# A transformer block on one core: two more tiles for exponentials, the first block's second layer in two parts, gated products for 256 rows, and a later use of turned rows

## The chip, the cores and the metric

The kernel runs on one core of a Trainium2 chip. The time is that of the device in microseconds. Three executions of the kernel before took 905.71, 910.32 and 911.77 us; their median is 910.32. A core has TensorE (PE, matmuls), VectorE (DVE), ScalarE (ACT), GpSimd (POOL) and SyncE (SP, which issues the transfers here).

## The reference

The input x has 2048 rows of 640 numbers. Attention has 32 heads of 20 numbers, and the second layer is a product of two linear maps of width 1728.

```python
qkv = (x @ wqkv).reshape(B, S, 3, H, Dh).transpose(2, 0, 3, 1, 4)
q, k, v = qkv[0], qkv[1], qkv[2]
p = softmax(einsum("bhqd,bhkd->bhqk", q, k) * Dh ** -0.5)
A = einsum("bhqk,bhkd->bhqd", p, v).transpose(0, 2, 1, 3).reshape(B, S, D) @ wo   # A(x, wqkv, wo)
Bf = ((x @ w_gate) * (x @ w_up)) @ w_down                                         # B(x, ...)
h = x + A(layernorm(x), wqkv, wo)
out = h + B(layernorm(h), w_gate, w_up, w_down)
```

## The kernel before

The 2048 rows are four blocks of 512 (`QB`), and each block is four row tiles of 128. First every row tile is normalized and turned, so that the 640 columns lie on partitions (`lnT`); from that come the keys `kT`, the queries `qa` and `qb`, and the values `vx`. For a block other than the first the turning is a DMA transpose, issued by `turn` (L892) as soon as the tile is normalized; `T_of` (L897) is a job that holds back the jobs behind it until the planner's clock has passed the issue by `TURN_NS`.

The attention is a train of 683 score tiles. `emit_S` (L521) writes one score tile `sc` in PSUM, 128 keys by 1536 columns, of which there are two. Each column group belongs to one head, one tile of keys and a block (or half a block) of queries. ScalarE takes the exponential of the tile into a tile `E` in SBUF (L551), out of a pool of `E_BUFS` = 6. In some tiles the last 512 columns are computed by VectorE instead, in four instructions (L587 to L598, `xe`). `emit_AV` (L739) then multiplies E with the values and sums in the one PSUM bank `acc`; a tile of E is free again when its last such matmul is done.

Everything else is a job: a generator that yields after each matmul. The kernel is written by a planner that runs while the program is built. It keeps an estimated clock for TensorE, ScalarE and VectorE (`at`), and between two score tiles `run_job` (L503) issues as many steps of the first job as fit, in the order of a queue. A job can yield `WAIT`, and then stands in `waiting` while the next is tried (`step`, L404). Where nothing is to be done, `keep_warm` (L494) issues two matmuls of 512 columns without use, and L531 one. Every engine then runs its list in order; semaphores alone decide the real times.

When all heads of a block (or of half a block) are normalized (`due`, L1365), `add_tail` (L1215) queues the rest for these rows. `job_out` (L1045) multiplies by `wo` (L1012), adds x, normalizes, and turns the rows by DMA into `ln2T` (L1058). `job_glu` (L1149) computes, for seven groups of 256 columns, the up product u and the gate product, and their product `hh`; for 512 rows at once in `glu_sum` (L1109) and for 256 rows in `glu_two` (L1124). `job_y` (L1172) multiplies by `w_down` (L1179), adds, and stores. Block 0 goes through this with 512 rows in one part, blocks 1 to 3 with 256 rows in two. `open_late` (L976) opens the pools for these tiles in the space of the turned rows, when no query or key is left to be computed. The weights `wu` and `wg` have two tiles each, and are fetched anew for each part; for block 3 four of the seven groups are kept in the space of the old queries. The queries are spilled to HBM (L970) for a general path that this input doesn't take. The last 256 rows follow behind the last exponential (`last_tail`, L1269).

Of the kernel before, what the change touches and what calls it, by code (L numbers as in the profile page):

```python
# [64 lines left out]
LN_NS = 3300  # L65
TURN_NS = 2600
HOLD_AT, HOLD_NS = 5300, 450
# [5 lines left out]
PART_NS, TILE_NS, ROOM = 31500, 700, 2500  # L73
E_BUFS = 6
SHIFT = 544.0
# [13 lines left out]
def kernel(  # L89
# [250 lines left out]
    FINAL = len(segs) - 1  # L340
    TAILS = {0: [0], 1: [0, 2], 2: [0, 2]}
    FAST = {("E", NG - 1), ("F", NG - 1), ("C", NG - 1), ("D", NG - 1), ("A", NG - 1), ("B", NG - 2)}
# [61 lines left out]
    def step():  # L404
        if cur["fresh"] and (first() or waiting):
            if cur["gen"] is not None:
                jobs.appendleft((cur["key"], cur["gen"]))
            cur["key"], cur["gen"] = (urgent if first() else waiting).popleft()
        c = advance()
        if c == WAIT:  # L410
            waiting.append((cur["key"], cur["gen"]))
            cur["gen"] = None
            c = advance() if jobs and not any(w[0][1:] == jobs[0][0][1:] for w in waiting) else NEXT
        if c is None:
            return None
# [87 lines left out]
    def run_job(until):  # L503
# [15 lines left out]
        return at["pe"] > begun  # L519

    def emit_S(i):  # L521
        sc = scp.tile([P, EW], F32, name="sc")
# [24 lines left out]
        if start <= at["exp"] + X_LATE and x_takes(i):  # L547
            n_act = n - BANK
            took = emit_x(sc[:, n_act:n], [(s, kt, j, o - n_act) for s, kt, j, o in us if o >= n_act])
        e = ep.tile([P, EW], BF16, name="E")  # L550
        exps = nc.scalar.activation(e[:, 0:n_act], sc[:, 0:n_act], ACT.Exp, bias=EXP_BIAS, scale=SM_SCALE)  # L551
# [162 lines left out]
    def av_ns(upto):  # L714
        if not av_q or acc["seg"] not in (None, av_q[0][1]):
            return 0
        s = av_q[0][1]
        if acc["seg"] is None and at["pe"] < at["acc"] and now["i"] < acc["from"] and min(u[0] for u in av_q) > now["i"] - E_BUFS:
            return 0
# [6 lines left out]
        left = acc["left"] if acc["seg"] == s else END_OF_TIME  # L726
        if sum(rows) < min(most * HPG, left) and min(u[0] for u in av_q) > upto - E_BUFS + 3:
            return 0
# [10 lines left out]
    def emit_AV(upto):  # L739
# [9 lines left out]
        if acc["seg"] != s:  # L749
            if at["pe"] < at["acc"] and now["i"] < acc["from"] and min(u[0] for u in av_q) > now["i"] - E_BUFS:  # L750
                return
# [8 lines left out]
        ready = sum(len(r) for r in rows)  # L760
        if ready < min(most, acc["left"]) and min(u[0] for u in av_q) > upto - E_BUFS + 3:
            return
# [105 lines left out]
    def gen_ln(ch):  # L868
# [8 lines left out]
        for k, t in enumerate(ts):  # L877
            apply1(t, *made[0], k)
            done.add(("a", t))
            later(1, lambda t=t: turn(t))  # L880
            yield 780
# [10 lines left out]
    def turn(t):  # L892
        if t not in turned:
            nc.sync.dma_start(lnT[:, :, t * P:(t + 1) * P], lns[t], transpose=True)
# [13 lines left out]

    for ch in range(NB):
        def values(k=0, n=TPB):  # L910
            for t in range(ch * TPB + k, ch * TPB + n):
# [9 lines left out]
        else:  # L921
# [54 lines left out]
    def open_late():  # L976
# [132 lines left out]
    def glu_sum(st, fp, f2, k, c0, n, hold):  # L1109
        ps = bank()  # L1110
        for c in range(KT):
            nc.tensor.matmul(ps[:, 0:n], lhsT=st["w", fp][k][:, c, f_cols(fp, f2)],  # L1112
                             rhs=st["ln2T"][:, c, c0:c0 + n], start=(c == 0), stop=(c == KT - 1))
            if c == KT - 1:
# [3 lines left out]
                else:  # L1118
                    dve(605 if n == QB else 342, 216 * n // QB)
                    nc.vector.tensor_tensor(st["hh"][fp][:, f2, c0:c0 + n], ps[:, 0:n], hold["u"][:, 0:n], ALU.mult)  # L1120
            yield 216 * n // QB
        yield NEXT

    def glu_two(st, fp, c0, n, up_done):  # L1124
        u = late["s"].tile([P, QB], BF16, name="u")
        for k in range(2):
            ps = bank()
            for f2 in range(2):
                for c in range(KT):
                    nc.tensor.matmul(ps[:, f2 * n:(f2 + 1) * n], lhsT=st["w", fp][k][:, c, f_cols(fp, f2)],  # L1130
                                     rhs=st["ln2T"][:, c, c0:c0 + n], start=(c == 0), stop=(c == KT - 1))
                    if f2 and c == KT - 1:
# [3 lines left out]
                        else:  # L1136
                            two = lambda x: x.rearrange("p (f k) -> p f k", k=n)
                            nc.vector.tensor_tensor(st["hh"][fp][:, :, c0:c0 + n], two(ps[:, 0:2 * n]), two(u[:, 0:2 * n]), ALU.mult)  # L1138
                    yield 216 * n // QB
# [32 lines left out]
    def job_y(st, ts, store_halves=False):  # L1172
        for t in ts:
            o = st["xr"][t]
            for hf in range(2):
                ps = bank()
                cs = slice(hf * HALF, (hf + 1) * HALF)
                for f in range(2 * FP):
                    nc.tensor.matmul(ps[:, 0:HALF], lhsT=st["hh"][f // 2][:, f % 2, t * P:(t + 1) * P],  # L1179
                                     rhs=late["Wd"][f][:, cs], start=(f == 0), stop=(f == 2 * FP - 1))  # L1180
# [13 lines left out]
    IN_TURN = (0, 3, 1, 4, 2, 5, 6)  # L1194
    tail_st = {}
    held = []

# [17 lines left out]
    def add_tail(b, ts):  # L1215
        key = (b, ts[0])

        def ready():
            if key not in rows_in:
                rows(b, ts)  # L1220
            if b == 0:
                for fp in range(2):
                    later(4 * fp + 3, lambda fp=fp: load_w(fp, tail_st[b]))
# [24 lines left out]
        if b == 0:  # L1248
            for g in range(NG):
# [110 lines left out]
    def normed(p, gs):  # L1360
# [3 lines left out]
    first_last = next(k for k, (us, _) in enumerate(tiles) if PASS[segs[us[0][0]][0]][0] == LAST_B)  # L1364
    due = [("0", range(NG), 0, [0, 1, 2, 3]), ("E", range(SPLIT_G["1"], NG), 1, [0, 1]), ("F", range(SPLIT_G["1"], NG), 1, [2, 3]), ("C", range(SPLIT_G["2"], NG), 2, [0, 1]),  # L1365
           ("D", range(SPLIT_G["2"], NG), 2, [2, 3]), ("A", range(SPLIT_G["3"], NG), 3, [0, 1])]
    PARTS = [d[2:] for d in due]
    i = 0
    while i < n_tiles or av_q:
# [15 lines left out]
        for _ in range(2):  # L1385
            emit_AV(i if i >= n_tiles else i - 2 if i >= LAG else i - 3)
            if not av_q or min(u[0] for u in av_q) > i - E_BUFS + 1:
                break
# [116 lines left out]
```

## Time and profile before

| | |
|---|---|
| median of three executions | 910.32 us (905.71 to 911.77) |
| the profiled execution | 910.77 us, span 909.0 us |
| TensorE matmuls | 830.1 us busy, 91% of the span |
| ScalarE | 855.7 us busy, 94% |
| VectorE | 757.0 us busy, 83% |
| exponentials on ScalarE (L551) | 683, 838.2 us |
| moved by DMA | 57.50 MB, 63 GB/s in the mean |

Busy time counts overlapping instructions of one engine once. The page cuts the span into 40 slices of 22.7 us and gives the busy share of each engine and the granted clock of TensorE in tenths. A timeline row merges like instructions that follow each other without a gap; its name is that of the first, so a row of 93 exponentials holds both those of 1536 and those of 1024 columns.

### The profile page before, as it was taken

Reading aid. Unit: us, or ns where it says so; the run is one execution under the profiler, and the core shown is the slowest. Engines: PE = TensorE matmul, PEld = TensorE weight load, DVE = VectorE, ACT = ScalarE, POOL = GpSimd, SP = SyncE. Lnnn points to the kernel's source line nnn. Section 1 sums busy time; section 2 is a strip of 40 time slices with the busy share of each in tenths; the row PEclk is TensorE's granted clock in tenths of the full one; section 3 lists DMA queues with packets and bytes.
Section 4 is the critical chain, followed back from the end, with each engine's and each line's share of the span. In section 5 each row is a group of like instructions: output and inputs, shape, how many; then the busy total and the mean of one; then the engine's idle time right before and its main releaser. Section 6 shows DMA issues by size and latency. Waiting matters only on the chain.

```text
span 909.0 us, 21597 instructions
## 1 busy us (share of the span) xinstructions
PE 830.1 (91%) x8766; PEld 364.3 (40%) x8766; DVE 757.0 (83%) x1411; ACT 855.7 (94%) x719; POOL 35.1 (4%) x126
## 2 busy tenths in 40 slices
PE   8889999989998899999999998998999999989997
PEld 5233233222233223344444454433434544435565
DVE  7668899999999798889888899899888898875543
ACT  6999999999999899999999999999989999999951
POOL 4100000000002000001001000000000000010000
PEclk9999999999999899999999999999989999999999
DMA  6230010011034235411415134111453202011310
GB/s 196 58 59 1 1 31 21 14 37 27 14 103 101 54 116 162 113 44 37 108 31 122 36 102 99 45 30 43 113 136 92 64 13 74 16 28 40 85 44 18
DMA packets 107578, 57.50 MB, mean 63 GB/s; under 512 B 41833, under 2 KB 104469, under 8 KB 107473
## 3 DMA queue, kind: packets, MB, share of 16 engines
q1 hardware_dynamic: 107472, 56.06, 23.9%
q8 instruction: 70, 1.15, 0.5%
q14 instruction: 36, 0.29, 0.1%
HBM read 44.49 MB, written 7.28 MB: 57 GB/s over the span
## 4 chain that ended last, share of the span: by engine, by line
ACT 49%; PE 27%; issue 13%; DVE 9%; DMA 1%; SPq 0%; ACTq 0%; DVEq 0%
ACT E L551 49%; PE mi L1130 6%; PE sc L535 6%; PE acc L772 5%; PE mi L303 2%; PE f L1112 2%; PE mi L1179 1%; PE mi L1112 1%; DVE xv L587 1%; PE f L1179 1%; DVE hh L1138 1%; DVE u L1135 1%; PE mi L498 1%; DMA ln2T<-ln 1%; DVE xt L597 1%
## 5 line engine op out<-in xcount | busy, mean ns | idle before, releaser
L551 ACT ACTIVATE E<-sc 128x1536 bf16<-128x1536 f32 (+1 forms) x683 | 838.2, 1396 | 15.5 <-PE sc L535 7.9
L535 PE MATMUL sc<-qa,kT 32*128 32x256 bf16 (+1 forms) x2176 | 204.0, 319 | 27.4 <-ACT E L551 20.7
L535 PEld LDWEIGHTS <-kT 32*128 32x128 bf16 x3136 | 87.0, 92 | 242.0 <-issue 211.7
L772 PE MATMUL acc<-E,vx 128*32 128x256 bf16 (+1 forms) x2833 | 170.1, 311 | 2.3 <-DVE asb L784 1.2
L587 DVE TENSOR_SCALAR xv<-sc 128x512 f32<-128x512 f32 x194 | 133.8, 690 | 45.5 <-PE sc L535 42.0
L592 DVE SCALAR_TENSOR_TENSOR xe<-xt,xv 128x512 int16<-128x512 f32 x194 | 131.6, 682 | 0.7
L598 DVE SCALAR_TENSOR_TENSOR xt<-xt,xv 128x512 f32<-128x512 f32 x194 | 130.9, 681 | 0.6
L597 DVE SCALAR_TENSOR_TENSOR xt<-xv 128x512 f32<-128x512 uint16 x194 | 130.7, 683 | 0.2
L772 PEld LDWEIGHTS <-vx 128*32 128x32 bf16 x3136 | 66.6, 96 | 71.5 <-issue 69.1
L303 PE MATMUL mi<-lnT,wp 128*128 128x512 bf16 x305 | 88.0, 386 | 7.0 <-DVE qa L310 3.1
L535 PE MATMUL sc<-qb,kT 32*128 32x256 bf16 (+1 forms) x960 | 69.3, 283 | 7.2 <-ACT E L551 6.2
L1179 PE MATMUL mi<-wd,hh 128*128 128x320 bf16 x364 | 64.2, 302 | 1.1 <-DVE xr L1183 1.0
L772 PE MATMUL acc<-xe,vx 128*32 128x256 bf16 (+1 forms) x303 | 63.9, 308 | 0.0
L1179 PEld LDWEIGHTS <-hh 128*128 128x128 bf16 x448 | 37.7, 98 | 29.8 <-issue 18.8
L303 PEld LDWEIGHTS <-wp 128*128 128x128 bf16 x310 | 24.9, 98 | 51.5 <-issue 40.2
L1130 PE MATMUL mi<-ln2T,wu 128*128 128x256 bf16 x270 | 39.2, 274 | 3.6 <-DVE hh L1138 3.5
L1012 PE MATMUL mi<-wo,on 128*128 128x320 bf16 x224 | 41.3, 307 | 0.6 <-DVE xr L1016 0.4
L1130 PE MATMUL mi<-ln2T,wg 128*128 128x256 bf16 x270 | 39.2, 274 | 2.9 <-DVE u L1135 2.4
L498 PE MATMUL mi<-kT,ident 128*128 128x512 bf16 x126 | 38.2, 385 | 1.6 <-DVE hh L1138 0.9
L1138 DVE TENSOR_TENSOR hh<-mi,u 128x512 bf16<-128x512 f32 x35 | 24.1, 688 | 12.0 <-PE mi L1130 11.9
L1135 DVE CAST u<-mi 128x512 bf16<-128x512 f32 x35 | 24.0, 687 | 11.6 <-PE mi L1130 11.2
L318 PE MATMUL mi<-wv,lnT 128*128 128x320 bf16 x160 | 29.3, 300 | 4.7 <-DVE vx L268 2.8
(142 smaller groups left out, 598.4 us busy)
## 6 DMA issues: line engine op xcount, KB each, us to landing
wu<-in_B_w_up_dram SPq DMA_DIRECT2D x32, 320.0 KB
wg<-in_B_w_gate_dram SPq DMA_DIRECT2D x32, 320.0 KB
bc<-scr SPq DMA_DIRECT2D x60, 64.0 KB
bc<-scr SPq DMA_DIRECT2D x108, 32.0 KB
qsp<-qa SPq DMA_DIRECT2D x8, 384.0 KB
xr<-in_A_x_dram SPq DMA_DIRECT2D x16, 160.0 KB
out_dram<-xr SPq DMA_DIRECT2D x14, 160.0 KB
wd<-in_B_w_down_dram SPq DMA_DIRECT2D x13, 160.0 KB
```

What stands on the lines that cost most here:

```text
L303: nc.tensor.matmul(ps[:], lhsT=wslice(m, g, c), rhs=lnT[:, c, ch * QB:(ch + 1) * QB], start=(c == 0), stop=(c == KT - 1))
L498: nc.tensor.matmul(ps[:], lhsT=ident[:], rhs=kT[0][:, 0:BANK], start=True, stop=True)
L535: nc.tensor.matmul(sc[:, o:o + w], lhsT=kT[g][SLOT * j:SLOT * (j + 1), kt * P:(kt + 1) * P], rhs=q_of(g, b, c0, w)[SLOT * j:SLOT * (j + 1) ...
L551: exps = nc.scalar.activation(e[:, 0:n_act], sc[:, 0:n_act], ACT.Exp, bias=EXP_BIAS, scale=SM_SCALE)
L587: took = nc.vector.tensor_scalar(v[:], ps, X_SCALE, X_BASE, ALU.mult, ALU.max)
L592: nc.vector.scalar_tensor_tensor(e[:], t[:], X_R, v[:], ALU.mult, ALU.add)
L597: lambda: nc.vector.scalar_tensor_tensor(t[:], u, X_P, u, ALU.add, ALU.mult),
L598: lambda: nc.vector.scalar_tensor_tensor(t[:], t[:], X_Q, u, ALU.add, ALU.mult),
L772: nc.tensor.matmul(acc["t"][SLOT * j:SLOT * (j + 1), 0:w], lhsT=vx[kt][:, VS * h:VS * h + SLOT], rhs=e, start=(acc["n"][j] == 0), stop=(ac ...
L1012: nc.tensor.matmul(ps[:, 0:HALF], lhsT=on[g][:, t * P:(t + 1) * P], rhs=wo[g][:, cs], start=(g == 0), stop=(g == NG - 1))
L1130: nc.tensor.matmul(ps[:, f2 * n:(f2 + 1) * n], lhsT=st["w", fp][k][:, c, f_cols(fp, f2)], rhs=st["ln2T"][:, c, c0:c0 + n], start=(c == 0), ...
L1179: nc.tensor.matmul(ps[:, 0:HALF], lhsT=st["hh"][f // 2][:, f % 2, t * P:(t + 1) * P], rhs=late["Wd"][f][:, cs], start=(f == 0), stop=(f == ...
```

## The change

It has four parts.

1. `E_LATE` = 2 more tiles for exponentials, `El`, in a pool of its own among the late ones, so from the moment at which `open_late` runs. From then on the ring is two El, then six E. Where the planner asked whether a tile of E is about to be needed, it now counts eight.
2. Block 0's second layer in two parts of 256 rows. Both are due at the same time. The products with `wo` of all four row tiles come first, then gate and up for tiles 0 and 1, their product with `w_down`, and then the same for tiles 2 and 3. The weights are fetched for each part.
3. `hh` holds 256 rows instead of 512, and both halves of a block use the same columns.
4. `TURN_NS` is 4200 instead of 2600, and `TURN_FROM` = 2: the rows of block 1 are turned by TensorE, and the turns are queued one behind the keys of head groups 2 and 3 of block 0 each, and two behind these. `step` now also sets aside a second job that has to wait.

```diff
-TURN_NS = 2600
+TURN_NS, TURN_FROM = 4200, 2
-E_BUFS = 6
+E_BUFS, E_LATE = 6, 2
...
             c = advance() if jobs and not any(w[0][1:] == jobs[0][0][1:] for w in waiting) else NEXT
+            if c == WAIT:
+                waiting.append((cur["key"], cur["gen"]))
+                cur["gen"], c = None, NEXT
...
+    def e_bufs():
+        return E_BUFS + E_LATE if "e" in late else E_BUFS
+
+    def new_e():
+        if "e" in late:
+            e_late["n"] += 1
+            if (e_late["n"] - 1) % (E_BUFS + E_LATE) < E_LATE:
+                return late["e"].tile([P, EW], BF16, name="El", tag="El")
+        return ep.tile([P, EW], BF16, name="E")
...
-        e = ep.tile([P, EW], BF16, name="E")
+        e = new_e()
...
-        if ready < min(most, acc["left"]) and min(u[0] for u in av_q) > upto - E_BUFS + 3:
+        if ready < min(most, acc["left"]) and min(u[0] for u in av_q) > upto - e_bufs() + 3:
...
-            later(1, lambda t=t: turn(t))
+            if ch >= TURN_FROM:
+                later(1, lambda t=t: turn(t))
...
+    def on_pe(t):
+        ensure_aux(("a", t))
+        yield from job_lnT(t)
...
+        nxt = deque(range((ch + 1) * TPB, (ch + 2) * TPB) if ch + 1 < TURN_FROM else [])
+
+        def one_T():
+            if nxt:
+                t = nxt.popleft()
+                add(("T", t), on_pe(t))
...
                 keys(g)
+                one_T()
+            one_T()
+            one_T()
         if ch + 1 < NB:
-            add(("T", 0, ch + 1), T_of(ch + 1))
+            if ch + 1 >= TURN_FROM:
+                add(("T", 0, ch + 1), T_of(ch + 1))
...
+        late["e"] = pool("le", E_LATE, side="right")
...
-    COLUMNS_OF = {(1, 0): (0, 0), (1, 2): (0, 0), (2, 0): (1, 0), (2, 2): (1, 2), (3, 0): (2, 0)}
+    COLUMNS_OF = {(1, 0): (0, 0), (1, 2): (0, 2), (2, 0): (1, 0), (2, 2): (1, 2), (3, 0): (2, 0)}
...
-                            nc.vector.tensor_tensor(st["hh"][fp][:, :, c0:c0 + n], two(ps[:, 0:2 * n]), two(u[:, 0:2 * n]), ALU.mult)
+                            nc.vector.tensor_tensor(st["hh"][fp][:, :, c0 % HW:c0 % HW + n], two(ps[:, 0:2 * n]), two(u[:, 0:2 * n]), ALU.mult)
...
-            st["hh"] = [late["h"].tile([P, 2, QB], BF16, name=f"hh{fp}") for fp in range(FP)]
+            st["hh"] = [late["h"].tile([P, 2, HW], BF16, name=f"hh{fp}") for fp in range(FP)]
...
+    due_0 = [2, 3]
...
             if b == 0:
+                rows(b, due_0)
...
-        if key in rows_in:
+        if key == (0, 2):
+            pass
+        elif key in rows_in:
             urgent.append(out)
...
             jobs.append(out)
+            if b == 0:
+                add(("out", 0, 2), lazy(lambda st: job_out(On, st, due_0, (0, 2))))
...
-    due = [("0", range(NG), 0, [0, 1, 2, 3]), ("E", range(SPLIT_G["1"], NG), 1, [0, 1]), ("F", range(SPLIT_G["1"], NG), 1, [2, 3]), ("C", range(SPLIT_G["2"], NG), 2, [0, 1]),
+    due = [("0", range(NG), 0, [0, 1]), ("0", range(NG), 0, [2, 3]), ("E", range(SPLIT_G["1"], NG), 1, [0, 1]), ("F", range(SPLIT_G["1"], NG), 1, [2, 3]), ("C", range(SPLIT_G["2"], NG), 2, [0, 1]),
```

More of the change, by code (lines that the diff above doesn't have):

```diff
@@ L340 @@
     FINAL = len(segs) - 1
-    TAILS = {0: [0], 1: [0, 2], 2: [0, 2]}
+    TAILS = {0: [0, 2], 1: [0, 2], 2: [0, 2]}
     FAST = {("E", NG - 1), ("F", NG - 1), ("C", NG - 1), ("D", NG - 1), ("A", NG - 1), ("B", NG - 2)}
@@ L519, in run_job @@
         return at["pe"] > begun
+    e_late = {"n": 0}
+    def e_bufs():
[6 more added lines that the diff above has]
+        return ep.tile([P, EW], BF16, name="E")
     def emit_S(i):
@@ L717, in av_ns @@
         s = av_q[0][1]
-        if acc["seg"] is None and at["pe"] < at["acc"] and now["i"] < acc["from"] and min(u[0] for u in av_q) > now["i"] - E_BUFS:
+        if acc["seg"] is None and at["pe"] < at["acc"] and now["i"] < acc["from"] and min(u[0] for u in av_q) > now["i"] - e_bufs():
             return 0
@@ L726, in av_ns @@
         left = acc["left"] if acc["seg"] == s else END_OF_TIME
-        if sum(rows) < min(most * HPG, left) and min(u[0] for u in av_q) > upto - E_BUFS + 3:
+        if sum(rows) < min(most * HPG, left) and min(u[0] for u in av_q) > upto - e_bufs() + 3:
             return 0
@@ L749, in emit_AV @@
         if acc["seg"] != s:
-            if at["pe"] < at["acc"] and now["i"] < acc["from"] and min(u[0] for u in av_q) > now["i"] - E_BUFS:
+            if at["pe"] < at["acc"] and now["i"] < acc["from"] and min(u[0] for u in av_q) > now["i"] - e_bufs():
                 return
@@ L1119, in glu_sum @@
                     dve(605 if n == QB else 342, 216 * n // QB)
-                    nc.vector.tensor_tensor(st["hh"][fp][:, f2, c0:c0 + n], ps[:, 0:n], hold["u"][:, 0:n], ALU.mult)
+                    nc.vector.tensor_tensor(st["hh"][fp][:, f2, c0 % HW:c0 % HW + n], ps[:, 0:n], hold["u"][:, 0:n], ALU.mult)
             yield 216 * n // QB
@@ L1178, in job_y @@
                 for f in range(2 * FP):
-                    nc.tensor.matmul(ps[:, 0:HALF], lhsT=st["hh"][f // 2][:, f % 2, t * P:(t + 1) * P],
+                    nc.tensor.matmul(ps[:, 0:HALF], lhsT=st["hh"][f // 2][:, f % 2, t * P % HW:t * P % HW + P],
                                      rhs=late["Wd"][f][:, cs], start=(f == 0), stop=(f == 2 * FP - 1))
@@ L1247, in add_tail @@
                 add(("y", b, t), lazy(lambda st, t=t: job_y(st, [t, t + 1])))
-        if b == 0:
+        if key == (0, 0):
             for g in range(NG):
@@ L1386 @@
             emit_AV(i if i >= n_tiles else i - 2 if i >= LAG else i - 3)
-            if not av_q or min(u[0] for u in av_q) > i - E_BUFS + 1:
+            if not av_q or min(u[0] for u in av_q) > i - e_bufs() + 1:
                 break
```

## The prediction

> **What bounds the kernel now.** I read the page first (busy shares, the granted clock by slices, the chain that ended last, the costliest groups), then what ScalarE and TensorE waited for.
>
> ```profile
> span 909.0 us, 21597 instructions
> ...
> PE 830.1 (91%) x8766; PEld 364.3 (40%) x8766; DVE 757.0 (83%) x1411; ACT 855.7 (94%) x719; POOL 35.1 (4%) x126
> ...
> PEclk9999999999999899999999999999989999999999
> ...
> ACT 49%; PE 27%; issue 13%; DVE 9%; DMA 1%; SPq 0%; ACTq 0%; DVEq 0%
> ...
> L551 ACT ACTIVATE E<-sc 128x1536 bf16<-128x1536 f32 (+1 forms) x683 | 838.2, 1396 | 15.5 <-PE sc L535 7.9 <-PE acc L772 7.3
> ```
>
> ScalarE is busy 855.7 of 909.0 us, and 838.2 us of that are the 683 exponentials of L551. In the whole train they waited 15.5 us. So the span is a sum with four terms: the time to the first exponential, 838.2 us of exponentials, 15.5 us of gaps, and what follows the last one. ScalarE's timeline gives the places (start, length, what, how many in a row, then in brackets the gap before and what ended it):
>
> ```profile
> 15.54 13.76 ACT L551 ACTIVATE E<-sc 128x1536 bf16<-128x1536 f32 x10 [0.66 <-PE sc L535]
> 30.35 12.20 ACT L551 ACTIVATE E<-sc 128x1536 bf16<-128x1536 f32 x9 [1.05 <-PE sc L535]
> 43.36 116.34 ACT L551 ACTIVATE E<-sc 128x1536 bf16<-128x1536 f32 x93 [0.82 <-PE sc L535]
> 160.14 145.52 ACT L551 ACTIVATE E<-sc 128x1536 bf16<-128x1536 f32 x120 [0.44 <-PE acc L772]
> 307.50 1.45 ACT L551 ACTIVATE E<-sc 128x1536 bf16<-128x1536 f32 x1 [1.84 <-PE sc L535]
> 310.19 47.05 ACT L551 ACTIVATE E<-sc 128x1536 bf16<-128x1536 f32 x39 [1.24 <-PE sc L535]
> 358.43 13.60 ACT L551 ACTIVATE E<-sc 128x1536 bf16<-128x1536 f32 x11 [1.19 <-PE acc L772]
> ...
> 664.04 1.45 ACT L551 ACTIVATE E<-sc 128x1536 bf16<-128x1536 f32 x1 [0.57 <-PE sc L535]
> 665.72 1.02 ACT L551 ACTIVATE E<-sc 128x1024 bf16<-128x1024 f32 x1 [0.24 <-PE sc L535]
> 668.26 85.12 ACT L551 ACTIVATE E<-sc 128x1536 bf16<-128x1536 f32 x70 [1.52 <-PE sc L535]
> ...
> 868.64 1.28 ACT L1382 ACT_TABLE_LOAD   x1
> ```
>
> The first exponential starts at 15.54 and the last ends by 868.64, so start and tail take 15.5 and 40.4 us, and only the gaps between can be moved by an edit to the middle. They are of two kinds.
>
> ```profile
> ACT E L551 <- PE sc L535: 7.9, 8, 1.8
> ACT E L551 <- PE acc L772: 7.3, 11, 1.2
> ```
>
> Eleven gaps, 7.3 us, ended with an `acc` matmul: the exponential wanted to write a tile of E whose old contents `acc` had not yet read. Eight, 7.9 us, ended with the scores themselves. Of these eight, the ones at 15.54 and 30.35 (0.66 + 1.05) are start-up. The other six stand where the granted clock falls, as windows of 5 us show (busy time with count of PE, PEld, DVE, ACT, POOL; then granted clock, DMA share, GB/s):
>
> ```profile
> 300.00:305.00 5.00, 3.15 (x24) 0.78 (x21) 4.80 (x8) 5.00 (x5) 0.00 (x0) 0.78 0.71 158
> 305.00:310.00 5.00, 5.00 (x22) 1.01 (x20) 2.49 (x4) 2.11 (x2) 0.00 (x0) 0.53 0.07 18
> 660.00:665.00 5.00, 4.36 (x23) 1.48 (x21) 3.39 (x8) 4.43 (x4) 0.00 (x0) 0.62 1.00 239
> 665.00:670.00 5.00, 5.00 (x32) 2.01 (x32) 3.88 (x7) 3.25 (x4) 0.00 (x0) 0.69 1.15 303
> 300.41 2.52 SPq L1058 DMA_TRANSPOSE ln2T<-ln  x2
> 304.56 2.29 PE L1112 MATMUL mi<-ln2T,wu 128*128 128x512 bf16 x5 [0.90 <-DMA ln2T<-ln]
> 30.61 5.68 SPq L894 DMA_TRANSPOSE lnT<-xs  x4
> 34.10 0.82 PE L303 MATMUL mi<-lnT,wp 128*128 128x512 bf16 x3
> 40.40 2.31 PE L303 MATMUL mi<-lnT,wp 128*128 128x512 bf16 x5
> 27.67 1.25 PE L303 MATMUL mi<-lnT,wp 128*128 128x512 bf16 x5
> ```
>
> The last two rows are the same five matmuls at half clock (2.31 us, just before the gap at 43.36) and at full clock (1.25). So three times TensorE ran at half speed and scores came late: 0.82 us at 43.36, 1.84 + 1.24 = 3.08 at 305 to 310, and 0.57 + 0.24 + 1.52 = 2.33 at 663 to 668; together 6.2. Each time few full-array matmuls had stood in the queue before: at 35 to 40 (none between 34.10 + 0.82 and 40.40) because chunk 1's rows were turned by four DMAs from 30.61 on, at 300 to 304 because the first block's second layer waited for turned rows (TensorE stood 0.90 us for that DMA), at 658 to 664 between two jobs.
>
> **The change part by part.**
>
> *What does not change.* The instruction order of both programs holds the same exponentials: 683, of which 195 leave 512 columns to VectorE. So 838.2 us stay.
>
> *Two more tiles of E.* I followed each tile of E in the order of TensorE's queue. With six tiles, 16 exponentials need a tile whose last `acc` matmul is queued behind their own scores, so they must wait for work that could not start earlier. With eight, from exponential 194 on (counted from 0), three are left, numbers 8, 48 and 112, all ahead of the new tiles; number 112 is the gap at 160.14, 0.44 us. So 7.3 - 0.44 = 6.9 us of gaps go. Ten exponentials in a row take 13.76 us where one takes 1.45: (13.76 - 1.45) / 9 = 1.37 from start to start, so a successor overlaps 0.08, and ten closed gaps give 0.8 more. I take **-7.7**; bounds 0 (scores come late in their place) and -7.7. Room for it in TensorE:
>
> ```profile
> PE sc L535 <- ACT E L551: 26.8, 62, 1.1
> ```
>
> TensorE waits 26.8 us for ScalarE to free score tiles; that is where the work of closed gaps comes from.
>
> *hh for 256 rows.* Same VectorE instructions. The second half now overwrites what the first half's L1179 matmuls read; these stand earlier in TensorE's own queue, and the gate and up matmuls that feed the overwriting multiply come behind them, so nothing new is waited for. Cost 0. If that order failed, VectorE would stand for the rest of a product row, by the tail's row below up to 1.52 us for ten matmuls, three times in the run.
>
> *First block in two parts.* 140 matmuls over 512 columns become 280 over 256.
>
> ```profile
> 656.63 1.14 PE L1130 MATMUL mi<-ln2T,wu 128*128 128x256 bf16 x9 [0.24 <-DVE hh L1138]
> wu<-in_B_w_up_dram SPq DMA_DIRECT2D x32, 320.0 KB
> 354.08 0.44 SPq L1078 DMA_DIRECT2D wu<-in_B_w_up_dram  x1
> 369.42 0.40 SPq L1078 DMA_DIRECT2D wu<-in_B_w_up_dram  x1
> 350.00:360.00 10.00, 8.93 (x96) 3.16 (x93) 9.16 (x16) 8.81 (x9) 0.00 (x0) 1.00 0.65 196
> PE mi L1112 <- DMA ln2T<-ln: 0.9, 1, 0.9
> ```
>
> Nine of 256 in 1.14 us are 0.13 each with their start-up, five of 512 in 1.25 are 0.25: 280 x 0.13 - 140 x 0.25 = +1.4 us of TensorE, inside the 26.8 us. The weights come in twice: 11 loads of 320 KB more on SP's queue, 0.4 us of issue each, ahead of nothing that ScalarE waits for. Now one pair of weights is fetched in about 15 us (354.08 to 369.42); afterwards in about half of that. Blocks 1 and 2 already run in halves, and among TensorE's 25 largest waits the last row is the only one of a matmul for a DMA in the second layer, so I take 0; the dear side is a rival below.
>
> *Later use of turned rows.* The planner now holds back work on DMA-turned rows 4200 instead of 2600 ns, so it fills the time with other matmuls and the 0.90 us stand at 304.56 should go, and the second layer starts on two row tiles, not four. I take the 3.08 us of that place as gone: **-3.1** (bounds 0 and -3.1). Chunk 1 is turned by TensorE: 20 transposes beside exponentials 10 to 18 and four VectorE copies, for four DMAs.
>
> ```profile
> L268 DVE COPY lnT<-acc 128x640 bf16<-128x640 bf16 x1 | 0.5, 491 | 0.6 <-PE acc L281 0.6
> 25.00:50.00 25.00, 20.79 (x151) 6.50 (x149) 17.59 (x44) 22.94 (x18) 2.34 (x7) 0.93 0.35 76
> ```
>
> Four copies at 0.49 us are 2.0 us, in a stretch in which VectorE is busy 17.59 of 25. In the old queue exponentials 14 to 17 have no full-array matmul beside them; in the new one 15 transposes stand beside 15 to 18, so I take the half clock at 40 as gone: **-0.8**; bounds 0 and -0.8. [...]
>
> *The clock elsewhere.* Neighbouring score tiles with under 600 columns of full-array work beside the two number 49 in the old order and 40 in the new; the old 49 gave three falls of the clock. 40 give 2.4. I keep the fall at 661 (2.33) and add one of the cheapest kind, 0.82: **+0.8**; bounds -2.3 (none at all) and +6.2 (two dear ones more, 3.08 each).
>
> *Tail.* Ten second-product matmuls used to stand between the last transposes and the first gate matmul; two do now.
>
> ```profile
> 878.75 1.52 PE L1179 MATMUL f<-wd,hh 128*128 128x320 bf16 x10
> 878.95 0.69 ACT L265 COPY ln2T<-acc 128x640 bf16<-128x640 bf16 x1 [0.55 <-PE acc L281]
> 880.11 4.09 PE L1112 MATMUL f<-ln2T,qa 128*128 128x256 bf16 x36
> ```
>
> The rows are ready at 878.95 + 0.69 = 879.64, used at 880.11: **-0.5**.
>
> Sum: -7.7 - 3.1 - 0.8 + 0.8 - 0.5 = -11.3; span 897.7. The profiled execution took 910.77, 1.8 outside its span, and stands 0.4 over the median of 910.32: **899.5 us**.
>
> **The rivals.**
>
> *The clock falls elsewhere.* [...] Two dear falls more: 899.5 + 6.2 = 905.7. [...] Against: the two places with named causes are treated.
>
> [...]
>
> *No fall at all.* Both -2.3 and no new one: 899.5 - 2.3 - 0.8 = 896.4.
>
> *The gaps only change their name.* If TensorE can't bring scores earlier, exponentials wait for `sc` where they waited for `acc`, and the 7.7 us stay: 907.2. Against: the 26.8 us above.
>
> *Weights late, slower.* In the first block a pair of 2 x 320 KB has some 7 us instead of 15, while the queries are spilled (L970). 350 to 360 moved 196 GB/s at a DMA share of 0.65; another 640 KB in 15 us are 43 GB/s, 239 in sum, which 660 to 665 moved at a share of 1.00. A late pair makes TensorE stand and the clock fall, as at 304.56, for 3.08 us. The gain is used up at four late pairs of 14; at eight it is 899.5 + 24.6 = 924. Against: spills lie beside only some four pairs in the new order.
>
> **How the numbers follow.** Forecast 0.42 (its own range 897 to 902), clock elsewhere 0.22, transposes 0.08, no fall 0.13, gaps renamed 0.08, weights late 0.07. A difference under 1% (901.2 to 919.4) is about what a measurement of this kernel can't tell from no change. Faster by more: no fall 0.13, most of forecast 0.32 and of the transposes' case 0.05, in sum 0.50; slower by more 0.06; within 1% 0.44. The range runs from 895 (no fall, with 1.4 to spare) to 908.5 (renamed gaps, with 1.3); over it lies the late-weights case, and some of the clock's.
>
> **What the profile after would show.** `E` waiting for `acc`: under 1 us in some three gaps, all before 170 us. PEclk with no digit under 9 near 40 and near 300. No wait of gate or up matmuls for DMA; one here, or of wu and wg, is the slower rival. L551 again x683 with 838 us. ScalarE's table load near 858. Wrong I'd be if waits for `sc` grew by what those for `acc` lose, or if new falls of the clock stood in the blocks that follow.

## The result, and the profile after

| | before | after |
|---|---|---|
| median of ten executions each | 910.39 us (905.71 to 913.35) | 898.74 us (895.98 to 904.27) |
| ratio, 95% interval | | 0.9892 (0.9867 to 0.9916) |
| the profiled execution, span | 910.77 us, 909.0 us | 895.98 us, 894.2 us |

The change takes 1.1% off. The profiled execution of after is the fastest of its ten; that matters below. Its page:

```profile
span 894.2 us, 21880 instructions
...
PE 800.1 (89%) x8861; PEld 373.1 (42%) x8919; DVE 760.1 (85%) x1415; ACT 853.5 (95%) x719; POOL 33.6 (4%) x126
...
PEclk9999999999999999999999999999999999999999
...
ACT 61%; PE 15%; issue 15%; DVE 9%; DMA 1%; ACTq 0%; DVEq 0%
...
L566 ACT ACTIVATE E<-sc 128x1536 bf16<-128x1536 f32 (+1 forms) x560 | 696.1, 1397 | 2.5 <-PE sc L550 1.7
...
L566 ACT ACTIVATE El<-sc 128x1536 bf16<-128x1536 f32 (+1 forms) x123 | 159.8, 1378 | 0.3 <-PE sc L550 0.3
```

The exponentials are the same 683 (560 into `E`, 123 into `El`), now on L566. They wait 2.8 us in all (2.5 + 0.3) where they waited 15.5, and ScalarE's share of the chain rises from 49% to 61% while TensorE's falls from 27% to 15%. No slice has a lowered clock. TensorE is busy for less, 800.1 against 830.1 us, with more matmuls. In before it ran at half clock for 17.1 us of the train, from 40.0, 302.8 and 661.2 on, which makes up at most 8.5 us of the 30; and the trace of after lacks the records of some matmuls (8919 weight loads, 8861 matmuls; in before 8766 of both), so its 800.1 is a little low.

The waits of ScalarE and of TensorE (us in total, times, longest):

```profile
ACT E L566 <- PE sc L550: 1.7, 2, 1.1
...
ACT E L566 <- PE acc L787: 0.4, 1, 0.4
...
PE sc L550 <- ACT E L566: 19.0, 50, 0.9
...
PE sc L550 <- ACT El L566: 5.0, 12, 0.9
...
PE mi L1162 <- DMA wg<-in_B_w_gate_dram: 0.5, 1, 0.5
```

The waits for `acc` went from 7.3 us in eleven to 0.4 in one, and those for `sc` from 7.9 to 2.0, of which 1.7 are start-up. TensorE has 24.0 us left of waiting for ScalarE. ScalarE's timeline, and TensorE's around the two old places and in the tail (start, length, what, how many; gap before):

```profile
16.05 13.76 ACT L566 ACTIVATE E<-sc 128x1536 bf16<-128x1536 f32 x10 [0.66 <-PE sc L550]
30.86 128.18 ACT L566 ACTIVATE E<-sc 128x1536 bf16<-128x1536 f32 x102 [1.05 <-PE sc L550]
159.47 99.60 ACT L566 ACTIVATE E<-sc 128x1536 bf16<-128x1536 f32 x82 [0.43 <-PE acc L787]
...
695.31 1.02 ACT L566 ACTIVATE El<-sc 128x1024 bf16<-128x1024 f32 x1 [0.25 <-PE sc L550]
...
854.24 1.28 ACT L1420 ACT_TABLE_LOAD   x1
864.93 0.69 ACT L265 COPY ln2T<-acc 128x640 bf16<-128x640 bf16 x1 [1.03 <-PE acc L281]
37.84 0.44 PE L281 MATMUL mi<-ident,xs 128*128 128x128 bf16 x5
42.23 1.24 PE L303 MATMUL mi<-lnT,wp 128*128 128x512 bf16 x4
864.73 0.43 PE L1211 MATMUL f<-wd,hh 128*128 128x320 bf16 x2
865.67 8.89 PE L1144 MATMUL f<-ln2T,qa 128*128 128x256 bf16 x80 [0.51 <-ACT ln2T L265]
```

Between 159.47 and the table load at 854.24 one gap with a length beside it is left, 0.25 us. Where the 14.8 us of span went: the idle of the exponentials -12.7 (15.5 to 2.8); the tail -0.4 (909.0 - 868.64 = 40.4 before, 894.2 - 854.24 = 40.0 after); the first exponential +0.5 (15.54 to 16.05). The rest, -2.2, is the fall of ScalarE's busy time from 855.7 to 853.5 us: exponentials that follow without a gap overlap (the ten from 16.05 on take 13.76 us, where one by itself takes 1.45, so 0.08 each), and overlapping time is counted once.

The median is 2.8 us above the profiled execution, and the granted clock says why. Each execution's mean clock is recorded with its time, and the clock records of all traces here hold full and half speed alone. So a mean of 0.990 in 904 us is 0.010 x 2 x 904 = 18 us at half clock; about 2 of them lie in the tail (2.0 in before, from 907.0 on, 2.2 in after), and are taken off in all that follows (the profiled execution after has 0.999, and its only fall is at 892.0). In this measure the 77 executions of the kernel before beside the experiments spent 12.1 us at half clock in the mean, and a straight line through time over half clock gives **0.34 us for each of these**, from 905.0 us at none. Single executions scatter about the line by 0.8 us (standard deviation), and the three groups of before that were taken beside the experiments give 904.9, 904.9 and 905.1 us at none. The ten of after spent 7.2 us: 895.98 and 896.55 at clock 0.999, 904.27 and 904.23 at 0.989 and 0.990. By the same 0.34 after stands at 896.9 without falls. So of the gain in the mean some 8 us are there without any fall, and 4.9 x 0.34 = 1.7 come from fewer of them.

### The profile page after: what moved, and what is told of

Its sections match the earlier page's. It is cut to its first block, busy times and chain, and to the rows that moved or that the text cites. A ratio compares the mean times of both kernels' runs of the same rounds, so it can differ in the third digit from the quotient of the medians.

```text
span 894.2 us, 21880 instructions
## 1 busy us (share of the span) xinstructions
PE 800.1 (89%) x8861; PEld 373.1 (42%) x8919; DVE 760.1 (85%) x1415; ACT 853.5 (95%) x719; POOL 33.6 (4%) x126
## 4 chain that ended last, share of the span: by engine, by line
ACT 61%; PE 15%; issue 15%; DVE 9%; DMA 1%; ACTq 0%; DVEq 0%
ACT E L566 49%; ACT El L566 11%; PE sc L550 3%; PE mi L1162 2%; PE acc L787 2%; PE f L1144 2%; PE mi L303 1%; DVE xv L602 1%; DVE xt L612 1%; PE f L1211 1%; DVE xt L613 1%; PE mi L1044 1%; DVE xe L607 1%; PE mi L318 1%; DVE u L1167 1%
## 5 line engine op out<-in xcount | busy, mean ns | idle before, releaser
L566 ACT ACTIVATE E<-sc 128x1536 bf16<-128x1536 f32 (+1 forms) x560 | 696.1, 1397 | 2.5 <-PE sc L550 1.7
L550 PE MATMUL sc<-qa,kT 32*128 32x256 bf16 (+1 forms) x2176 | 203.0, 318 | 27.9 <-ACT E L566 14.8
L566 ACT ACTIVATE El<-sc 128x1536 bf16<-128x1536 f32 (+1 forms) x123 | 159.8, 1378 | 0.3 <-PE sc L550 0.3
L787 PE MATMUL acc<-E,vx 128*32 128x256 bf16 (+1 forms) x2255 | 156.9, 314 | 1.2 <-DVE vx L268 0.6
L1162 PE MATMUL mi<-ln2T,wg 128*128 128x256 bf16 x390 | 56.7, 274 | 8.6 <-DVE u L1167 7.6
L1162 PE MATMUL mi<-ln2T,wu 128*128 128x256 bf16 x390 | 55.7, 274 | 7.2 <-DVE hh L1170 7.0
L787 PE MATMUL acc<-El,vx 128*32 128x256 bf16 (+1 forms) x579 | 59.5, 292 | 0.3 <-ACT El L566 0.3
L787 PE MATMUL acc<-xe,vx 128*32 128x256 bf16 (+1 forms) x302 | 55.4, 306 | 0.3 <-issue 0.3
L1162 PEld LDWEIGHTS <-wg 128*128 128x128 bf16 x390 | 33.7, 97 | 30.0 <-issue 25.9
L1162 PEld LDWEIGHTS <-wu 128*128 128x128 bf16 x390 | 33.7, 97 | 28.3 <-issue 25.2
L1170 DVE TENSOR_TENSOR hh<-mi,u 128x512 bf16<-128x512 f32 x49 | 33.7, 688 | 13.3 <-PE mi L1162 12.7
```

What stands on the lines that cost most here:

```text
L550: nc.tensor.matmul(sc[:, o:o + w], lhsT=kT[g][SLOT * j:SLOT * (j + 1), kt * P:(kt + 1) * P], rhs=q_of(g, b, c0, w)[SLOT * j:SLOT * (j + 1) ...
L787: nc.tensor.matmul(acc["t"][SLOT * j:SLOT * (j + 1), 0:w], lhsT=vx[kt][:, VS * h:VS * h + SLOT], rhs=e, start=(acc["n"][j] == 0), stop=(ac ...
L1170: nc.vector.tensor_tensor(st["hh"][fp][:, :, c0 % HW:c0 % HW + n], two(ps[:, 0:2 * n]), two(u[:, 0:2 * n]), ALU.mult)
```

## The experiments

They ask which part brought it, since the prediction gave 7.7 of its 11.3 us to waits for tiles of E, 3.1 to the later use of turned rows and 0.8 to the transposes. "Half clock" and "without falls" are worked out as above, with 0.34 for all; the last column is the largest stand of second-layer matmuls for turned rows (`ln2T`) in the profile. In the row of before, half clock and without falls are those of the 77 executions. Each ratio is to executions of before that were taken beside it on the same chip, whose medians were 908.54, 909.18 and 909.43 us for the experiments.

| kernel | median us (n) | ratio to before, 95% | half clock us | without falls us | wait for `acc` us | stand us |
|---|---|---|---|---|---|---|
| before | 910.39 (10) | | 12.1 | 905.0 | 7.3 | 0.9 |
| after | 898.74 (10) | 0.9892 (0.9867 to 0.9916) | 7.2 | 896.9 | 0.4 | none |
| after, six tiles | 910.47 (12) | 1.0016 (0.9994 to 1.0037) | 15.9 | 905.3 | 1.8 | 2.0 |
| after, ring of eight, six counted | 908.62 (12) | 0.9997 (0.9975 to 1.0019) | 17.4 | 903.4 | 0.4 | 2.2 |
| after, seven tiles | 903.17 (5) | 0.9923 (0.9896 to 0.9950) | 11.0 | 899.5 | 0.4 | 0.5 |
| after, `TURN_NS` 2600 | 908.49 (10) | 0.9998 (0.9979 to 1.0018) | 18.0 | 902.7 | 0.4 | 3.1 |
| after, block 1 turned by DMA | 901.95 (5) | 0.9903 (0.9871 to 0.9936) | 14.2 | 896.9 | 0.4 | none |
| before + parts 2, 3 | 907.62 (12) | 0.9974 (0.9953 to 0.9995) | 5.9 | 905.4 | 1.2 | 0.2 |
| before + `TURN_NS` 4200 | 910.74 (12) | 1.0026 (1.0007 to 1.0045) | 19.0 | 904.9 | 4.0 | 1.5 |
| before + transposes for block 1 | 910.68 (10) | 1.0012 (0.9986 to 1.0038) | 13.3 | 905.6 | 7.2 | 0.7 |

### After with six tiles

```diff
-E_BUFS, E_LATE = 6, 2
+E_BUFS, E_LATE = 6, 0
...
-        late["e"] = pool("le", E_LATE, side="right")
```

> The changed kernel without the two El tiles; the other three parts stay. In the order of the queues 11 exponentials (8, 48, 112, 219, 262, 304, 326, 443, 475, 592, 624, counted from 0) stand behind an acc matmul that is queued behind their own scores, against 3 with El; and VectorE takes 512 columns of 191 tiles, not of 195. Theory (the two tiles are what saves): about 8 gaps ended by acc come back at 0.7 us, and 4 tiles at 0.43 us more on ScalarE: 898.7 + 5.6 + 1.7 = about 906, in the profile ScalarE waiting some 5 to 7 us for acc. Rival (the gaps before were the clock's, and the other parts saved): 899 to 900, with under 2 us of waits for acc.

It takes the whole gain away: 910.47 us. But not through the waits for tiles. The waits of this kernel, and its TensorE at two places:

```profile
ACT E L566 <- PE sc L550: 7.1, 10, 1.5
ACT E L566 <- PE acc L787: 1.8, 4, 0.6
...
PE mi L1161 <- DMA ln2T<-ln: 2.5, 2, 2.0
...
444.24 0.81 PE L1161 MATMUL mi<-ln2T,wu 128*128 128x256 bf16 x6 [2.02 <-DMA ln2T<-ln]
875.99 2.88 PE L1210 MATMUL f<-wd,hh 128*128 128x320 bf16 x20
```

The waits for `acc` are 1.8 us, 1.4 above after, where the expectation had 5 to 7 from its count of eleven exponentials behind their own last `acc` matmul in the queue. The waits for `sc` are 7.1: up to 444.24 TensorE stood 2.02 us for turned rows, from 445.5 on it ran 10.2 us at half clock, and ScalarE has four gaps of 1.45, 1.06, 0.68 and 1.11 us between 444 and 456. In the tail 20 second products, not 2, stand behind the last transposes (2.88 us), and from the last exponential to the end it takes 42.6 us against 40.0. VectorE shares 191 tiles, not 195: four more exponentials of the long kind, 1.45 against 1.02 us each, 1.7 in sum. With a count of six the planner wrote another program.

### After with a ring of eight, of which the planner counts six

```diff
     def e_bufs():
-        return E_BUFS + E_LATE if "e" in late else E_BUFS
+        return E_BUFS
```

> The changed kernel with the two El tiles in the ring, but the planner still counts six, so every queue holds the same instructions in the same order as in the kernel with six tiles (median 910.5), and only the waits for a tile of E get looser: 3 exponentials instead of 11 behind their own acc matmul. Theory A (the tiles save by removing waits): most of the 11.7 us between six and eight tiles comes back, about 901 to 903. Theory B (waits for acc were only 1.8 us in that kernel; the tiles save by what the planner does when it may count eight: VectorE takes 195 tiles and not 191, the tail is 40.0 and not 42.6 us, the clock falls less): only about 2 us, 908 to 909, with the tail at 42.6 and some 14 us at half clock as before.

This separates the two things that part 1 does. Every engine's list is that of the kernel with six tiles; only the tile that is written differs. The waits for `acc` fall to 0.4, as in after, and the time is 908.62, by the two ratios 0.0019 x 909 = 1.7 us below the six tiles, which is less than its uncertainty (about 2.8 us, from the two intervals); without falls it is 1.9. So the ring itself is worth some 2 us under this order, and the other 9.5 (0.9997 against 0.9892) hang on what the planner writes when it counts eight. Whether the order for eight would run as well on a ring of six was not run. The stand at 444 is still there:

```profile
443.77 1.44 PE L1162 MATMUL mi<-ln2T,wu 128*128 128x256 bf16 x6 [2.22 <-DMA ln2T<-ln]
```

The clock falls from 442.7 on, while TensorE stands, for 13.7 us. The 6.5 us without falls between this kernel and after (903.4 to 896.9) agree with what the two profiles show: 2.5 us for ScalarE's gap at this stand, 2.4 for the tail (42.4 against 40.0), and 1.7 for the four more exponentials of the long kind, 6.6 in sum. (The gap holds a part of the fall; in the kernel with six tiles, where the clock fell later, it is 1.45, which would make 5.6.)

### After with seven tiles

```diff
-E_BUFS, E_LATE = 6, 2
+E_BUFS, E_LATE = 6, 1
```

> The changed kernel with one El tile, ring and planner at seven: 5 exponentials behind their own acc matmul, VectorE takes 191 tiles. Theory A (waits): 2 gaps more than with eight, 1.4 us, and 1.7 us for the four tiles: 902. Theory B (what the planner does): no smooth step with the number of tiles, the time goes by the plan: with 191 tiles as with six, near 905 to 908.

903.17 us, between the two values expected. The waits for `acc` are as low as with eight (0.4 us) and no gate or up matmul stands more than 0.5 us for its rows, but the list of the tail is that with 20 second products, 42.4 us long. That tail is 2.4 us, and the 191 shared tiles are 1.7 more on ScalarE as with six; together they are more than the 2.6 us by which it stands above after without falls. With five executions that figure is uncertain by about 0.9, and what makes up the difference isn't shown.

### After with the old hold of turned rows

```diff
-TURN_NS, TURN_FROM = 4200, 2
+TURN_NS, TURN_FROM = 2600, 2
```

> The changed kernel with 2600 ns for a turned row. VectorE takes 196 tiles, 3 exponentials behind their own acc. If 4200 ns carry a part of the gain, TensorE waits for turned rows again in the first block, and the time is 900 to 902; if they only shift the plan, 898 to 899.5 without such waits.

908.49 us: again the gain is gone, and by more than either expectation had. The waits of TensorE, ScalarE's and TensorE's timeline:

```profile
PE mi L1162 <- DMA ln2T<-ln: 3.1, 1, 3.1
...
811.25 1.14 PE L1162 MATMUL mi<-ln2T,wu 128*128 128x256 bf16 x9 [3.08 <-DMA ln2T<-ln]
812.84 2.37 ACT L566 ACTIVATE E<-sc 128x1024 bf16<-128x1024 f32 x2 [2.94 <-PE sc L550]
816.15 2.79 ACT L566 ACTIVATE E<-sc 128x1536 bf16<-128x1536 f32 x2 [0.95 <-PE sc L550]
```

The work on turned rows is released 3.08 us too early, not in block 0 but at 811 us in block 3, and costs 2.94 + 0.95 us of gaps. The same kernel has the 20 products in its tail (42.4 us). With both gaps that is 3.9 + 2.4 = 6.3 us; the second gap lies behind a fall of the clock from 812.7 on for 3.4 us, and without it the sum is 5.3. The kernel lies 5.8 above after without falls; more time at half clock (18.0 against 7.2 us, 3.7 by 0.34) is the rest.

### The kernel before with the new hold alone

```diff
-TURN_NS = 2600
+TURN_NS = 4200
```

> The kernel before with the planner's time for a turned row at 4200 ns, not 2600, alone. The prediction's step: TensorE's stand of 0.90 us for turned rows goes and with it the fall of the clock near 303 us, -3.1: about 906 to 907. Rival (the fall there comes from the thin stretch before, which stays; and the plan behind it is another: 12 exponentials behind their own acc and not 16, VectorE takes 192 tiles and not 195): 908 to 910, with a fall near 300 still there in the profile or not by chance.

910.74 us, no gain, and by the ratio 0.3% slower if anything. Its TensorE at the old place:

```profile
304.99 1.24 PE L1112 MATMUL mi<-ln2T,wu 128*128 128x512 bf16 x5 [1.15 <-DMA ln2T<-ln]
```

The stand for turned rows is still there, 1.15 us where it was 0.90, and yet the five matmuls behind it ran at full clock (1.24 us, in the kernel before 2.29). So the longer hold does not cure this stand, and the stand alone does not make the clock fall. A second stand, of 1.47 us, lies at 817 us.

### The kernel before with parts 2 and 3 alone

It is after with `E_BUFS, E_LATE = 6, 0`, without the late pool, and `TURN_NS, TURN_FROM = 2600, 1`. It keeps the change to `step`.

> The kernel before with the first block's second layer in two parts and gated products for 256 rows alone: six tiles of E, turning as before (2600 ns, block 1 by DMA). 10 exponentials behind their own acc matmuls against 16 before, 191 tiles shared with VectorE against 195. Theory: these two parts are there to make room for El and save little: 6 gaps fewer (-4.3 us), 4 tiles more on ScalarE (+1.7), falls of the clock as before: about 907 to 909. Rival (the first block's smaller parts are what saves, since they let the second layer start early and keep the clock up): 900 to 902.

907.62 us, 0.3% under before. The waits of TensorE show what cured the stand of block 0:

```profile
PE mi L1161 <- DMA wg<-in_B_w_gate_dram: 0.7, 1, 0.7
...
PE mi L1161 <- DMA ln2T<-ln: 0.2, 1, 0.2
```

With the products by `wo` for all four row tiles ahead and the second layer beginning on two of them, nothing stands at 304 with the old 2600. The weights that come twice cost one stand of 0.7 us in the run. Without falls the kernel is at 905.4, where before is at 905.0: what it gains are falls (5.9 against 12.1 us). Its profile nevertheless has one at 40.5, for 13.7 us. That no time is won without falls is a balance: with six tiles still, the waits for `acc` are 1.2 us in place of 7.3, but the tail takes 42.7 us in place of 40.4, and VectorE shares 191 tiles, which is 1.7 us more for ScalarE. The rest of the balance isn't accounted for.

### The kernel before with transposes for block 1, and after without them

```diff
-TURN_NS = 2600
+TURN_NS, TURN_FROM = 2600, 2
...
-            later(1, lambda t=t: turn(t))
+            if ch >= TURN_FROM:
+                later(1, lambda t=t: turn(t))
...
-            add(("T", 0, ch + 1), T_of(ch + 1))
+            if ch + 1 >= TURN_FROM:
+                add(("T", 0, ch + 1), T_of(ch + 1))
```

(and `on_pe` and `one_T` as in the change; the reverse experiment is `TURN_FROM = 1` in after)

> The kernel before with block 1's rows turned by TensorE alone. The instructions from the 40th score tile on are those of before. Theory (transposes hold the clock as other matmuls do): no slice or window under full clock between 34 and 45 us, the gap of 0.82 us at 43.4 is gone, 16 exponentials still behind acc with some 7 us of waits: 909.5, 0.8 under the kernel before. [...]

> The changed kernel with block 1's rows turned by DMA as before, and the planner's 4200 ns for them. No exponential more behind acc than in the changed kernel. Theory: TensorE's clock falls to half near 36 to 43 us in every execution, ScalarE loses 0.8 to 1.5 us there and nothing elsewhere: 899.5 to 900.2 against 898.7. Rival (TensorE's transposes only move work): no fall there, 898.7.

On the kernel before no gain can be seen (910.68 us); the 0.8 us that were expected lie within the interval. ScalarE's timeline of that kernel:

```profile
30.89 128.18 ACT L551 ACTIVATE E<-sc 128x1536 bf16<-128x1536 f32 x102 [1.05 <-PE sc L535]
...
307.32 1.45 ACT L551 ACTIVATE E<-sc 128x1536 bf16<-128x1536 f32 x1 [2.00 <-PE sc L535]
```

The gap at 43 is gone as in after, the one at 307 stayed, with a fall of the clock from 301.1 on for 6.8 us, and another fell from 775.6 on for 10.2 us in place of that at 661.

After with the DMA turns is at 901.95 us, 3.2 above after, with intervals that overlap; without falls both are at 896.9. Its TensorE, and windows of 5 us (busy time with count of PE, PEld, DVE, ACT, POOL; clock, DMA share, GB/s):

```profile
34.66 0.82 PE L303 MATMUL mi<-lnT,wp 128*128 128x512 bf16 x3
...
42.13 1.25 PE L303 MATMUL mi<-lnT,wp 128*128 128x512 bf16 x4
...
35.00:40.00 5.00, 3.02 (x31) 0.73 (x29) 2.05 (x5) 5.00 (x5) 1.96 (x6) 1.00 0.48 80
40.00:45.00 5.00, 2.85 (x25) 0.99 (x23) 3.25 (x10) 5.00 (x5) 0.00 (x0) 1.00 0.32 117
```

From 34.66 + 0.82 to 42.13, 6.6 us, TensorE ran score and `acc` matmuls alone, as at 35 to 40 in before, and the clock stayed at 1.00. So a stretch of that kind does not always bring a fall. Before and the two kernels that kept its turns in this stretch (with parts 2 and 3, and with `TURN_NS` 4200) fell between 38.7 and 40.5; this one did not; it fell from 289.1, 398.3, 654.3 and 770.4 on, and the fall near 40 that was expected in every execution is not there. That after and the kernel before with transposes show none there is in favour of the transposes, but one execution each doesn't show it by itself.

### The falls that are left: no warming, more warming

Three kernels ask what the falls are worth. One is after without the matmuls of `keep_warm` (126) and of the line ahead of a score tile (18), whose results nothing reads:

```diff
     def keep_warm(...):
...
-        ps = bank()
-        for _ in range(2):
-            nc.tensor.matmul(ps[:], lhsT=ident[:], rhs=kT[0][:, 0:BANK], start=True, stop=True)
...
-            nc.tensor.matmul(sc[:, 0:BANK], lhsT=ident[:], rhs=kT[0][:, 0:BANK], start=True, stop=True)
```

> The changed kernel without the planner's matmuls without use: 126 of L501 and 18 of L546 are left out, their places in the plan stay. The result is unchanged, since nothing reads them. Theory (thin places let the clock fall, and each us at half clock costs 0.34): some 25 windows of 3.4 us, 60 to 90 us at half clock, 896.5 + 20 to 30 = 917 to 927. Rival (the clock follows something else and the filler is a burden on TensorE): 896 to 900.

912.88 us, ratio 1.0039 (1.0019 to 1.0060), 14.1 above after. Its clock by slices, and TensorE's largest waits:

```profile
PEclk9999999999998999999799999985999999969999
...
PE sc L546 <- ACT E L562: 40.7, 90, 1.2
PE sc L546 <- ACT El L562: 13.6, 23, 1.3
```

It spends 95.7 us at half clock, at the upper end of what was expected, but the time is 4 us under the expected 917 to 927: the 88.5 us more cost 0.16 us each, half of the price found on the kernel before. A line through its own ten executions gives 0.16 as well (with an uncertainty of 0.08), so the price is not lowered by the work that was left out. TensorE still waits 54.3 us for ScalarE in this kernel; how much of the half clock lies in such spare time isn't shown.

The other two add one filler of 512 columns ahead of chosen score tiles of after: in thin places, with little work on the whole array, of which the list names 35 and the trace shows 29 (at the others the kernel has a matmul of its own), and in 15 where TensorE had at least 0.3 us to spare. The edit with the 15:

```diff
+FILL = {196, 217, 218, 221, 223, 225, 306, 307, 340, 475, 487, 563, 609, 631, 638}
...
+        elif i in FILL:
+            nc.tensor.matmul(sc[:, 0:BANK], lhsT=ident[:], rhs=kT[0][:, 0:BANK], start=True, stop=True)
```

> The changed kernel with 29 or so matmuls of 512 columns more ahead of score tiles, at places where the trace of the changed kernel shows little full-array work in 3.4 us; the planner's clock does not see them, so all else stands in the same order. Theory (TensorE at half clock costs 0.34 us per us, by 30 executions of the kernel before, and thin places cause it): time at half clock falls from 7.2 us in the mean to 2 to 3, the median from 898.7 to 897, the slowest from 904.3 to under 900. Rival (the falls are not made by thin places): 898.7 to 900 with the same spread, or more, since 29 x 0.2 us are added to TensorE.

> The changed kernel with 15 matmuls of 512 columns without use, each at a place where the trace of the changed kernel shows TensorE idle for 0.3 us or more ahead of the scores, chosen where little full-array work stands in 3.4 us. Theory (29 such matmuls took the falls of the clock away but cost 2.6 us, because most stood where TensorE had no time to spare): falls mostly gone, 2 to 3 us at half clock in the mean and not 7, no cost beside: 897.0 to 897.8, slowest under 902. Rival (each costs by itself, 0.09 us as in the kernel with 29): 898.7 to 899.5, no gain.

The 29 fillers bring 899.13 us, ratio 0.9876 (0.9848 to 0.9903): four of five executions have clock 0.999 and lie between 898.82 and 899.69, so the falls are nearly gone (1.4 us at half clock), but without falls the kernel is at 899.1, 2.2 over after. What the falls cost (7.2 - 1.4 = 5.8 us of them, 2.0 by 0.34), the fillers cost. The 15 bring 900.02, ratio 0.9910 (0.9882 to 0.9939), with 4.9 us at half clock and 899.3 without. Neither is better than after, and the 897 to 898 of the two expectations did not come. Why 15 fillers in places with time to spare cost as much as 29 isn't shown.

## Why the prediction was right, point by point

The forecast of 899.5 us is 0.8 over the median, in its own range of 897 to 902. Its last step names 0.4 us between the profiled execution and the median and doesn't take them off; with them it is 899.1. In the two profiles the time went where the sum said: out of the gaps for `acc` (6.9 us), out of those for `sc` (5.9) and out of the tail. The prediction had in part wrong which part of the change closes a gap; where one of its terms fits for another reason than the one given, that is luck. Terms measured by undoing one part at a time can't be added up, since the parts need each other: the tiles and the longer hold, each undone alone, are 8.4 and 5.8 us without falls, and the whole change is 8.1.

**Two more tiles, -7.7.** The size fits: after against six tiles is -8.4 us without falls, and -1.2% in all. Waits for `acc` fell as told, 7.3 to 0.4 us, the last one at 159.47. The cause is only partly right. The step read the eleven waits of the old order as the price of six tiles, and with parts 2 to 4 in place six tiles have only 1.8 us of them, with parts 2 and 3 alone 1.2. The two tiles themselves, under one order, brought 1.9 us without falls. The rest of the 8.4 hangs on the count of eight, by the order that the planner writes: no stand of 2 us for turned rows at 444, four more tiles shared with VectorE, a tail 2.6 us shorter. The step put nothing on any of these, so the fit of 7.7 and 8.4 is luck. That the orders with six are worse for one reason in common isn't shown.

**Overlap of closed gaps, 0.08 each.** Too small: ScalarE's busy time fell by 2.2 us over the fifteen gaps above 0.15 us that went (18 to 3), about 0.15 each.

**`hh` for 256 rows, first block in two parts, 0.** Right in sum: 905.4 against 905.0 us without falls for these parts alone, though as a balance of fewer waits for `acc` with a longer tail and fewer shared tiles, which the step didn't have. The rival of late weights fell: one stand of 0.5 us for weights in after, 0.7 in the parts alone.

**Turned rows, -3.1.** The stand and the gaps at 305 are gone, but the step credited `TURN_NS` first and the start on two row tiles beside it, and the runs credit the latter: with 4200 alone the stand stays (1.15 us), with the two parts (and the change to `step`) it is gone at 2600. What 4200 does for after was not in the prediction: it prevents a stand of 3.08 us at 811 and keeps the short tail, 5.8 us without falls.

**Chunk 1 turned by TensorE, -0.8.** The gap at 43 went in both kernels with transposes. By the median the step is worth 3.2 us in after with much uncertainty, all of it falls, and nothing on the kernel before. After has 15 transposes from 37.84 to 41.65 between two groups of full-array matmuls and a clock of 1.00. A stretch without any of them kept its clock as well (after with DMA turns, 6.6 us at 1.00), so that the transposes held it up isn't shown.

**The clock elsewhere, +0.8.** In the median it fits, but not as places: the step kept the fall at 661, and the profiled execution of after has no fall in the train at all (the rival of 896.4; it took 895.98). Five others, from 898.19 to 899.65, had a clock of 0.995, some 7 us at half clock, and two 0.99 and 904.2, as the rival of falls elsewhere (905.7) has it. These are executions of one kernel, not separate outcomes. In the mean, falls brought 1.7 us, where the three terms on the clock (-3.1, -0.8, +0.8) add up to 3.1. The +0.8 was an estimate from a count of places, 49 and 40; no run shows that falls go by that count.

**Tail, -0.5.** Measured 0.4: the rows are ready at 864.93 + 0.69 = 865.62 and used at 865.67, a delay of 0.05 us where it was 0.47.

**Gaps renamed.** Not in after (waits for `sc` 2.0 us), and not with six tiles either: 1.8 for `acc`, and 7.1 for `sc` where before had 7.9.

## What to carry to other kernels

Where a planner writes the order, a buffer count is also one of its inputs: run the count and the buffers apart before saying that a wait for a buffer was the cost. An edit that gains nothing alone (the longer hold), or little (the extra tiles without it), can be what another needs, so undo parts from the full change as well as adding them to the old kernel. And when single profiles differ by a clock that falls at one place or another, compare the times over their mean granted clock first, and read the places last.

## What the runs showed of the hardware

In these kernels, which ScalarE bounds (busy 94% of the span in before, 95% in after), a microsecond of TensorE at half clock costs 0.34 us when there are some 12 of them (77 executions of before) and 0.16 when there are some 95 (the kernel without warming). Falls inside the train lasted 3.4 us (before, from 40.0 on), 6.8 (before, from 302.8 and from 661.2 on), 10.2 (after with six tiles, from 445.5 on) and 13.7 (after with a ring of eight, from 442.7 on). Executions of one program differ: the ten of after have mean clocks from 0.989 to 0.999.

What decides whether the clock falls, the runs answer in part. In the mean, more matmuls of 512 columns on the whole array went with less time at half clock: after spends 95.7 us of it without those whose results nothing reads, 7.2 with them, 4.9 with 15 more and 1.4 with 29 more. For a single stretch that doesn't hold. In before TensorE was at work with score and `acc` matmuls alone from 34.92 to 40.40, and the clock fell from 40.0 on; after with DMA turns had the same matmuls alone for 6.6 us, up to 42.13, and kept 1.00. After and the kernel before with transposes for block 1 had transposes there and kept 1.00 from 35 to 45, which the kernel with DMA turns did without them. Nor is a stand of TensorE enough: behind 0.90 us at 304.56 in before five matmuls took 2.29 us, and behind 1.15 us at 304.99 in before with `TURN_NS` 4200 they took 1.24. Why the clock fell in one such stretch and not in another isn't shown.
